# Two 1024-wide products in a row over neighbouring PSUM banks, and TensorE's order as a written list

## The chip, the cores and the metric

The kernel runs on one core of a Trainium2 chip. The metric is the device time of one execution in microseconds (us). A core has five engines with a queue of instructions each: TensorE (PE in the profile, with its weight loads as PEld), VectorE (DVE), ScalarE (ACT), GpSimd (POOL) and SyncE (SP, which issues transfers here). Each engine takes its queue in order; an instruction can wait for events of other engines, and then everything behind it on that engine waits too.

## The reference

Two stages. The first is attention through 32 inducing points, the second a gated feed-forward layer on its result.

```
x: 4 x 12416 x 128     inducing: 32 x 128
mab(q, kv): a = softmax(q @ kv.T / sqrt(128)) ; return a @ kv
h   = mab(inducing, x)          # 32 x 128 for each of the 4 batches
y   = mab(x, h)                 # 12416 x 128 for each batch
out = (sigmoid(y @ w_gate) * (y @ w_val)) @ w_out
                                # w_gate, w_val: 128 x 1536, w_out: 1536 x 128
```

## The kernel before

The attention weights of a token over the 32 inducing points are called a2. Since y = a2 @ h, the kernel never forms y: for each batch it makes hw, that is h @ w_gate and h @ w_val (32 rows each), and a hidden value is a2 @ hw, a matmul that contracts over 32 rows. The sigmoid is written as (1 + tanh(g/2)) / 2.

The unit of the main loop is a **chunk**: 512 tokens (one of 97 blocks) by 128 hidden columns (one of 12). A chunk needs a matmul for the gate (`g_ps`, 128x512 in PSUM), a matmul for the value (`v_ps`), ScalarE's tanh of the gate (`t`), VectorE's product u = (t + 1) * v, which reads `v_ps` straight from PSUM, and four 128x128 matmuls of u with w_out that add into `acc_ps`. When the 12 chunks of a block are in, ScalarE copies `acc_ps` out times one half (`o`), and SP sends it. There are 1164 chunks; 9 of the last batch go *aside* (tanh and copy on ScalarE, product on GpSimd), so VectorE makes 1155.

Chunks go in **steps** that alternate between two chunks and one. PSUM has eight banks of 512 fp32 columns: two for a double gate, one for a single gate, two for a double value, one for a single value, one for `acc_ps`, and one, `m`, that everything else shares in turn. So VectorE's products alternate between 128x1024 and 128x512. Two steps, three chunks, are a **slot**.

The order around them is written by a Python loop, the same for every step t: `product(t)` issues the value matmuls of step t, behind them the gate matmuls of step t + 2, then the product; `gate(t + 2)` issues the tanh; at odd t `project` issues 12 or 16 of the output matmuls. Other work is hung on slot numbers by `at(slot, make)`. It is: stage 1 for the next batch (scores of the inducing points over x, max, exp, sums), joining the groups into h and hw, and stage 2 (scores s2, their exponentials `e`, GpSimd's sums and inverse, the spread `a2n`, and a transposing transfer `a2r` that the gate and value matmuls of 48 chunks read). A stage 2 table entry gives the slots of its scores, of ScalarE's copy `sc`, and of its exponential.

Gate and value matmuls of a chunk sit in different row tiles of the array: rows 0 to 63 hold the gate's (even and odd hidden column blocks 32 rows each), rows 64 to 127 the value's. A product of two chunks has a no-op ahead of it on VectorE that takes its wait for the tanh.

Of the kernel before, what the change touches and what calls it, by code (L numbers as in the profile page):

```python
# [16 lines left out]
P = 128  # L18
GC = 16
BC = 4  # L20
ASIDE = {3: ((2, 9, 3, 8), (11, 17, 7, 1), (23, 26, 7, 0), (50, 53, 15, 3), (58, 62, 19, 11), (64, 69, 19, 10), (73, 76, 20, 5), (78, 81, 23, 11), (83, 88, 23, 10))}
LATE = (4, 19, 32, 46, 43)
# [11 lines left out]
TINY = 1.0e-9 / P  # L34


@with_exitstack
def kernel(
# [31 lines left out]
    up = ctx.enter_context(tc.tile_pool(name="up", bufs=6))  # L70
    tp = ctx.enter_context(tc.tile_pool(name="tp", bufs=4))
    op = ctx.enter_context(tc.tile_pool(name="op", bufs=4))
# [145 lines left out]

    summed = [0] * B
    def keep_on(n, tag):  # L220
# [9 lines left out]
    plan = {}  # L230

    def at(slot, make, late=False, side=False):
        plan.setdefault((slot, "side" if side else late), []).append(make)
# [15 lines left out]
    def s1_score_pe(b, s, tag, s1=None):  # L249
        c0, n = groups[s]  # L250
        ng, w, R = s1_dims(s)
        if s1 is None:
            s1 = ps.tile([P, 512], F32, tag=tag, name="s1_ps")
        for g in range(ng):
            nc.tensor.matmul(  # L255
                s1[32 * g : 32 * g + 32, 0 : w * P],
                indT[:],
                xT[b][:, c0 + g * w : c0 + (g + 1) * w, :].rearrange("c j t -> c (j t)"),
                start=True,
                stop=True,  # L260
            )
        return s1

    def s1_max(b, s, s1):
        ng, w, R = s1_dims(s)
        nm, _, col = s1_col(b, s)
        nc.vector.tensor_reduce(  # L267
            out=nm[0:R, col], in_=s1[0:R, 0 : w * P], axis=AX.X, op=ALU.max, negate=True
        )
# [6 lines left out]
    def s1_exp(b, s, s1):  # L276
# [3 lines left out]
        nc.scalar.activation(  # L280
# [5 lines left out]
        )  # L286
        return a1T

    def s1_turn_pe(b, s, a1T, tag="m"):
        ng, w, R = s1_dims(s)  # L290
        aT = ps.tile([P, 4, P], F16, tag=tag, name="aT_ps")
        for k in range(w):
            nc.tensor.transpose(aT[:, k, 0:R], a1T[0:R, ts(k, P)], ident[0:R, 0:R])
        return aT

    def s1_turn_copy(s, aT):
        ng, w, R = s1_dims(s)
        a1 = s1p.tile([P, 4, P], F16, tag="a1")
        nc.vector.tensor_copy(out=a1[:, 0:w, 0:R], in_=aT[:, 0:w, 0:R])
# [7 lines left out]
    def s1_sum_pe(b, s, a1, hp, k0, k1):  # L307
        c0, n = groups[s]
        ng, w, R = s1_dims(s)
        for k in range(k0, min(k1, w)):  # L310
            for cols, src in ((slice(0, C), None), (slice(C, C + 1), ones16[:])):
                for g in range(ng):
                    if b == 0 and src is not None:
                        continue
                    nc.tensor.matmul(  # L315
# [6 lines left out]
                    )  # L322

    def s1_sum_keep(b, s, hp):
# [5 lines left out]
        nc.scalar.copy(out=hsts[b % 2][0:R, at_col[s], 0:width], in_=hp[0:R, 0:width])  # L330

    def plan_stage1(b, s, score, total):
        st = {}
        full = groups[s][1] == GC

        def begin():
            st["s1"] = s1_score(b, s, "m")

        def weigh():
            st["a1T"] = s1_exp(b, s, st["s1"])  # L340

        def turn():
            if full:
                st["a1"] = s1_turn_dma(b, s, st["a1T"])
            else:
                st["a1"] = s1_turn_copy(s, s1_turn_pe(b, s, st["a1T"]))

        at(score, begin)
        at(score + 1, weigh, late=full)
        at(score + 2, turn)  # L350
        first, second, keep = total

        def part(k0, k1):
            if k0 == 0:
                st["hp"] = ps.tile([P, C + 1], F32, tag="m", name="hp_ps")
            s1_sum_pe(b, s, st["a1"], st["hp"], k0, k1)

        at(first, lambda: part(0, 2))
        at(second, lambda: part(2, 4))
        at(keep, lambda: s1_sum_keep(b, s, st["hp"]))  # L360
# [12 lines left out]
    def l_inverse(l_ps):  # L373
        li = bp.tile([P, m], F32, tag="li")
        nc.vector.reciprocal(out=li[:], in_=l_ps)
        return li

    def h_take(b, h_ps, li):
        hT16[b] = bp.tile([P, m], F16, tag="hT", name="hT")
        nc.vector.tensor_tensor(out=hT16[b][:], in0=h_ps, in1=li[:], op=ALU.mult)  # L380

    def hw_fill(b, hf, tag):
        hw_ps = ps.tile([P, NI // 2, P], F32, tag=tag, name="hw_ps")
        for r in range(4):
            wsrc = wg16 if r < 2 else wv16
            nc.tensor.matmul(
# [5 lines left out]
            )  # L392
        return hw_ps
# [22 lines left out]
    def plan_combine(b, lead, weights, fill):  # L416
# [4 lines left out]
        def least():  # L421
# [3 lines left out]
            st["col"] = join_min(bp, ml)  # L425
# [27 lines left out]
        def total():  # L453
            lh = ps.tile([P, 2, m], F32, tag="m", name="lh_ps")
            nc.tensor.matmul(lh[:, 0, :], ones[:], st["e32l"][:], start=True, stop=True)
            nc.tensor.matmul(lh[:, 1, :], st["hx"][:, 0, 0:C], e32[:], start=True, stop=True)
            st["lh"], st["li"] = lh, l_inverse(lh[:, 0, :])

        def part(hf):
            st["hw_ps"] = hw_fill(b, hf, "m")  # L460

        def keep(hf):
            if hf == 0:
                st["hwt"] = bp.tile([P, NI, P], F16, tag="hw", bufs=B, name="hwt")
            nc.scalar.copy(out=st["hwt"][:, ts(hf, NI // 2), :], in_=st["hw_ps"][:])
# [3 lines left out]
        at(lead, least)  # L469
        at(weights, weigh)  # L470
        at(weights + 1, join)
        at(weights + 8, total)
        at(weights + 9, lambda: h_take(b, st["lh"][:, 1, :], st["li"]))
        for hf, (first, second) in enumerate(fill):
            at(first, lambda hf=hf: part(hf))
            at(second, lambda hf=hf: keep(hf), late=True)
# [4 lines left out]
    def s2_score(b, c, j0, j1, s2, whole=False):  # L481
        for j in range(j0, j1):
            nc.tensor.matmul(  # L483
# [6 lines left out]
            )  # L490

    def s2_max(n, s2):
        nmx = s2p.tile([P, GC], F32, tag="nmx")
        nc.vector.tensor_reduce(
            out=nmx[:, 0:n], in_=s2[:, 0:n, :], axis=AX.X, op=ALU.max, negate=True
        )
# [8 lines left out]
    def s2_exp(n, s2, hi, lo):  # L505
        for t_, last in ((hi, False), (lo, True)):
            nc.tensor.matmul(
# [6 lines left out]
            )  # L514
        e = s2p.tile([P, GC + NLO, m], F16, tag="e")
        nc.scalar.activation(out=e[:, 0:n, :], in_=s2[:, 0:n, :], func=AF.Exp, scale=SCALE)
        return e

    def s2_take(sc, c0, n, s2):
        nc.scalar.copy(out=sc[:, c0 : c0 + n, :], in_=s2[:, 0:n, :])  # L520
# [96 lines left out]
    def plan_stage2(b, c, score, take, weigh, far=None, soon=False):  # L617
        st = {}
        n = GC + (NLO if far is not None else 0)

        def bank():
            st["s2"] = ps.tile([P, GC, m], F32, tag="m", name="s2_ps")
# [4 lines left out]
        def one():  # L627
            room()
            bank()
            s2_score(b, 0, 0, NLO, st["s2"], True)  # L630

        def half(j0, whole):
            if j0 == 0:
                bank()
            s2_score(b, c, j0, j0 + GC // 2, st["s2"], whole)
            if soon and j0:
                st["hl"] = s2_max(GC, st["s2"])

        def lower():
            if far is None:  # L640
                room()
            s2_take(st["sc"], 0, GC, st["s2"])
            s2_lower_pool(n, st["sc"])

        def exp():
            st["e"] = s2_exp(GC, st["s2"], *st["hl"]) if soon else s2_exp_low(n, st["sc"])

# [12 lines left out]
        if far is not None:  # L660
            at(far, one)
            at(far + 1, lambda: s2_take(st["sc"], GC, NLO, st["s2"]))
        at(score, lambda: half(0, False))
        at(score + 1, lambda: half(GC // 2, not soon))
        if not soon:
            at(take, lower, late=True)
        at(weigh, exp, late=True)
        at(weigh + 1, total)
        at(weigh + 3, spread)
        at(weigh + (5 if soon else 8 if far is None else 7), turn)  # L670
# [187 lines left out]
    s2_a = ps.tile([P, GC, m], F32, tag="m", name="s2_ps")  # L858
# [34 lines left out]
    a2T = [ps.tile([P, half, P], F16, tag=t, name="a2T_ps") for t in ("m", "v1")]  # L893
# [17 lines left out]
    steps = []  # L911
    blocks = []
    first_step = {}
    for b in range(B):
        for s in range(NG):
            first_step[(b, s)] = len(blocks) * 2 * NJ // 3
            blocks += [[(b, groups[s][0] + k, BC)] for k in range(0, GC, BC)]
    blocks.append([(b, 0, NLO) for b in range(B)])
    order = [list(range(NJ)) for _ in blocks]
    aside = []  # L920
    for b, table in ASIDE.items():
        first = b * NG * GC // BC
        for g, v, i, j in table:
            order[first + i].remove(j)
            aside.append((first * 4 + g, first * 4 + v, first + i, j))
    for i in range(len(blocks)):
        js = list(order[i])
        while js:
            cnt = 1 if steps and steps[-1]["cnt"] == 2 else 2
# [261 lines left out]
```

## Time and profile before

| | |
|---|---|
| median of 3 runs | 719.6 us (719.52 to 720.22) |
| span of the profiled execution | 718.4 us; the median of the runs is 1.2 us longer, taken as what lies around the span |
| VectorE busy | 702.4 us (98%), 872 instructions |
| ScalarE busy | 675.1 us (94%), 1019 instructions |
| TensorE busy (matmul) | 650.5 us (91%) |
| GpSimd busy | 445.8 us (62%) |
| products on VectorE | 385 of 128x1024, 384 of 128x512, the last cut in two |

The page gives no other time for the profiled execution than its span, so sums are made against the span plus 1.2 us. Busy time of an engine is the union of its instructions; the mean length of one instruction is longer than its share of that, where each begins before the one ahead of it has ended. "Idle before" in a group's row is the time in which the engine did nothing just ahead of these instructions, with what ended most of it.

### The profile page before, as it was taken

What the parts mean: (1) busy time and instruction counts of PE and PEld (TensorE: products, weight loads), DVE (VectorE), ACT (ScalarE), POOL (GpSimd) and SP (SyncE); (2) the same over time, 40 slices, a digit from 0 to 9 for tenths busy, and PEclk for the clock granted to TensorE, in tenths of its full rate; (3) what the DMA queues carried; (4) which work ended last, traced back from release to release, by engine and by line L of the source; (5) the groups of instructions that cost most, each with busy time, mean ns of one, the idle gap of its engine ahead of it and who ended that gap; (6) DMA issues with size and microseconds to landing.
All of it is one profiled execution on the core that took longest, in us unless ns stands there. A gap on an engine that the chain in (4) does not pass through costs nothing.

```text
span 718.4 us, 21566 instructions
## 1 busy us (share of the span) xinstructions
PE 650.5 (91%) x8446; PEld 394.2 (55%) x8446; DVE 702.4 (98%) x872; ACT 675.1 (94%) x1019; POOL 445.8 (62%) x718
## 2 busy tenths in 40 slices
PE   8889889999998998999989988999899999999897
PEld 4455555555555555555555555555555555555555
DVE  5899999999999999999999999999999999999997
ACT  4699999999999999999999999999999999999996
POOL 4574763888653747588666266387766787676220
PEclk9999999999999999999999999999999999999999
DMA  9796696244568344335268431220222122223011
GB/s 209 115 182 130 125 165 105 75 90 106 89 133 162 80 103 92 59 79 119 66 117 161 102 75 51 70 74 31 77 60 73 46 62 67 39 75 71 35 46 46
DMA packets 118182, 65.77 MB, mean 92 GB/s; under 512 B 101408, under 2 KB 102208, under 8 KB 118080
## 3 DMA queue, kind: packets, MB, share of 16 engines
q1 hardware_dynamic: 112176, 50.90, 31.6%
q0 software_dynamic: 5584, 13.34, 10.9%
q8 instruction: 66, 1.08, 0.6%
q14 instruction: 36, 0.29, 0.1%
q10 hardware_dynamic: 320, 0.15, 0.1%
HBM read 27.80 MB, written 25.43 MB: 74 GB/s over the span
## 4 chain that ended last, share of the span: by engine, by line
PE 51%; ACT 24%; DVE 16%; issue 5%; DMA 2%; DVEq 1%; POOL 1%; ACTq 0%
PE acc_ps L1062 24%; ACT t L962 22%; PE v_ps L944 21%; DVE u L981 14%; PE g_ps L944 2%; DMA xn<-in_x_dram 2%; PE s_ps L483 2%; PE hp_ps L315 1%; ACT o L1081 1%; DVE nm L267 1%; DVEq L981 1%; ACT a1T L280 0%; PE s_ps L255 0%; POOL xn L96 0%; ACTq L962 0%
## 5 line engine op out<-in xcount | busy, mean ns | idle before, releaser
L981 DVE SCALAR_TENSOR_TENSOR u<-t,v_ps 128x1024 f16<-128x1024 f16 (+1 forms) x771 | 670.9, 945 | 1.7 <-PE g_ps L944 0.8
L962 ACT ACTIVATE t<-g_ps 128x1024 f16<-128x1024 f32 (+1 forms) x770 | 589.5, 822 | 22.2 <-ACT t L962 10.3
L944 PE MATMUL v_ps<-a2r,hwt 32*128 32x512 f16 (+1 forms) x1179 | 290.8, 371 | 56.9 <-DVE u L981 53.2
L1062 PE MATMUL acc_ps<-wo,u 128*128 128x128 f16 x4620 | 324.5, 220 | 0.9
L1062 PEld LDWEIGHTS <-u 128*128 128x128 f16 x4620 | 259.9, 98 | 89.5 <-issue 88.1
L944 PE MATMUL g_ps<-a2r,hwt 32*128 32x512 f16 (+1 forms) x1179 | 294.0, 376 | 0.0
L944 PEld LDWEIGHTS <-hwt 32*128 32x128 f16 x2382 | 93.5, 91 | 188.6 <-issue 142.2
L552 POOL TENSOR_TENSOR sum<-e 128x256 f32<-128x256 f16 (+1 forms) x23 | 15.5, 672 | 133.8 <-ACT e L544 130.0
L598 POOL TENSOR_TENSOR a2n<-e,rs 128x2048 f16<-128x2048 f16 (+3 forms) x25 | 86.8, 3474 | 4.8 <-DVE rs L570 3.1
L576 POOL TENSOR_TENSOR near<-sme,minus 128x16 f32<-128x16 f32 (+1 forms) x22 | 65.3, 2966 | 1.8
L1081 ACT ACTIVATE o<-acc_ps 128x512 f32<-128x512 f32 x96 | 58.4, 609 | 0.0
L531 POOL TENSOR_SCALAR rise<-rise 128x256 f32<-128x256 f32 (+6 forms) x110 | 51.2, 466 | 9.7
L532 POOL TENSOR_TENSOR top<-top,rise 128x128 f32<-128x128 f32 (+3 forms) x88 | 28.4, 323 | 7.3
L552 POOL TENSOR_TENSOR sum<-sum 128x128 f32<-128x128 f32 (+3 forms) x92 | 28.4, 309 | 7.2
L530 POOL TENSOR_TENSOR rise<-top 128x128 f32<-128x128 f32 (+3 forms) x88 | 27.3, 310 | 6.9
L530 POOL TENSOR_TENSOR rise<-sc 128x256 f32<-128x256 f32 (+1 forms) x22 | 16.3, 739 | 20.9 <-ACT sc L520 20.6
L1031 POOL TENSOR_TENSOR xn_spare<-xn_spare 128x512 f16<-128x512 f32 x9 | 11.4, 1270 | 22.2 <-ACT xn_spare L1029 22.0
L535 POOL TENSOR_TENSOR sc<-sc,top 128x512 f32<-128x512 f32 (+1 forms) x22 | 23.9, 1086 | 1.7
L1026 POOL TENSOR_SCALAR xn_spare<-xn_spare 128x512 f32<-128x512 f16 x9 | 13.4, 1493 | 11.2 <-ACT xn_spare L1025 11.2
L483 PEld LDWEIGHTS <-xT 128*128 128x128 f16 x388 | 13.1, 96 | 11.7 <-issue 11.3
L280 ACT ACTIVATE a1T<-s_ps,nm 128x512 f16<-128x512 f32 (+1 forms) x26 | 16.4, 630 | 3.1 <-DVE nm L267 3.0
L483 PE MATMUL s_ps<-hT,xT 128*128 128x32 f16 x388 | 18.1, 178 | 0.1
(150 smaller groups left out, 291.4 us busy)
## 6 DMA issues: line engine op xcount, KB each, us to landing
out_dram<-o SPq DMA_DIRECT2D x96, 256.0 KB, 2.2
xn<-in_x_dram POOLq DMA_DIRECT2D x18, 512.0 KB, 7.7
xn<-in_x_dram POOLq DMA_DIRECT2D x3, 544.0 KB, 6.9
xn<-in_x_dram POOLq DMA_DIRECT2D x3, 256.0 KB, 12.8
xn<-in_x_dram SPq DMA_DIRECT2D x1, 576.0 KB, 4.8
xn<-in_x_dram SPq DMA_DIRECT2D x1, 512.0 KB, 3.9
a2r<-a2n SPq DMA_TRANSPOSE x29, 4.5
wg<-in_moe_w_gate_dram POOLq DMA_DIRECT2D x1, 384.0 KB, 12.7
```

The lines of the kernel that those rows point to most:

```text
L483: nc.tensor.matmul(s2[:, j, :], xT[b][:, c + j, :], hT16[b][:], start=(j == 0), stop=whole and j == j1 - 1, skip_group_check=True,)
L530: nc.gpsimd.tensor_tensor(out=r, in0=far, in1=near, op=ALU.subtract)
L531: nc.gpsimd.tensor_scalar_max(out=r, in0=r, scalar1=0.0)
L532: nc.gpsimd.tensor_tensor(out=top[:, 0:n, 0:w], in0=near, in1=r, op=ALU.add)
L552: nc.gpsimd.tensor_tensor(out=d[:, 0:n, :], in0=src[:, :, 0:w], in1=src[:, :, w : 2 * w], op=ALU.add)
L576: nc.gpsimd.tensor_tensor(out=near[:, 0:n], in0=sme[:, 0:n], in1=minus1[:, 0:n], op=ALU.pow)
L598: eng.tensor_tensor(out=a2n[:, 0:n, :, :], in0=e.unsqueeze(2).to_broadcast((P, n, 4, m)), in1=rs.unsqueeze(2).unsqueeze(3).to_broadcast((P ...
L944: st[what + "end"] = nc.tensor.matmul(pt[:, k, col : col + nb * P], hw[b][r : r + 32, j // 2, :], a2r[r : r + 32, o : o + nb, :].rearrange ...
L962: st["tanh"] = nc.scalar.activation(out=st["t"][:], in_=st["g"][:], func=AF.Tanh, scale=0.5)
L981: u = nc.vector.scalar_tensor_tensor(out=st["u"][:, :, c:e], in0=st["t"][:, :, c:e], scalar=1.0, in1=st["v"][:, :, c:e], op0=ALU.add, op1= ...
L1062: nc.tensor.matmul(acc[0][(i // 2) % len(acc[0])][:, i, :], u[:, ts(i, P)], wo16[:, j, :], start=(i in fresh), stop=not any(e[2] == ib and ...
L1081: nc.scalar.mul(out=o32[:], in_=acc[0][0][:], mul=0.5)
```

## The change

Bank `m` and the single value bank become one tile `vm` of two neighbouring banks. In a slot in which no other work holds `m`, the second product is 128x1024 over both banks of `vm`; in the others it is 128x512 in the first bank, and `m` serves as before. Words in a long text, `ORDER`, now say what is issued next: `V` or `W` value matmuls (a `W` at a slot's start makes its second product wide), `x` the product, `g` a gate's matmuls with its tanh, `o8` eight output matmuls, `p`, `a` and `d` other work on TensorE, ScalarE and VectorE. Gates still alternate between two chunks and one, and their tanh goes into one ring of 16 chunks. Blocks begin with even or odd hidden columns in turn so that pairs fit. Slots in the tables (`TIMES`) become chunk positions (three per slot), and several moved by one or two; the nine aside chunks stay nine, from other places of the order. Buffers for u go from 18 chunks to 16, those for the copied-out block from 4 to 3. `on` tells the scheduler that users of one bank of `vm` need not wait for users of the other.

```diff
+    vm.append(ps.tile([P, 2, 512], F32, tag="vm", name="vm_ps"))
...
-    def product(t):
-        st = steps[t]
-        hidden_mm(st, "v")
...
-        gate_fill(t + 2)
-        if t % 2:
-            beside(t // 2, "side")
...
+    def fill_value():
+        c, n, half = value["chunk"], sizes[value["step"]], value["step"] % 2
+        if half == 0:
+            turn_page(c)
+        v = vm[0] if half else ps.tile([P, 2, 512], F32, tag="v2", name="v_ps")
+        for k in range(n):
...
+            for i in hidden_mm("v", c + k, v[:, k, :]):
...
+    def product():
...
+        cuts = [0, 384, 512] if final else [0, 512]
+        for a, e in zip(cuts, cuts[1:]):
+            x = nc.vector.scalar_tensor_tensor(
+                out=u[:, 0:n, a:e],
+                in0=ring[:, p : p + n, a:e],
+                scalar=1.0,
+                in1=v[:, 0:n, a:e],
...
+ORDER = """
+ggVxggVxpVxgVxo4ggVxgVxpo12gVd0xo8go4gVxo4Vxgo4a0gVxo8Wxo4a0gVxgo12gWxo4gVxo12gVxgo8pgVxpo4a0gWx
...
+    for word, k in words:
+        if word in "VW":
+            fill_value()
+        elif word == "x":
+            product()
+        elif word == "g":
+            issue_gate()
+        elif word == "o":
+            for _ in range(int(k)):
+                out_mm()
+        else:
+            run(later[{"p": "pe", "a": "act", "d": "dve"}[word]].pop(int(k or 0)))
```

VectorE's queue in the second batch of tokens, before: u is the product, t the tanh, and the size is that of the result.

```order
L981 SCALAR_TENSOR_TENSOR u_3341<-t_3311,v_ps 128x512
L981 SCALAR_TENSOR_TENSOR u_3365<-t_3335,v_ps 128x1024
L981 SCALAR_TENSOR_TENSOR u_3395<-t_3343,v_ps 128x512
L981 SCALAR_TENSOR_TENSOR u_3417<-t_3368,v_ps 128x1024
L981 SCALAR_TENSOR_TENSOR u_3434<-t_3397,v_ps 128x512
```

And a like stretch of VectorE's queue with the change; `t_621` is the ring.

```order
L1350 SCALAR_TENSOR_TENSOR u_3323<-t_621,vm_ps 128x1024
L1350 SCALAR_TENSOR_TENSOR u_3337<-t_621,v_ps 128x1024
L1350 SCALAR_TENSOR_TENSOR u_3368<-t_621,vm_ps 128x512
L1350 SCALAR_TENSOR_TENSOR u_3386<-t_621,v_ps 128x1024
L1350 SCALAR_TENSOR_TENSOR u_3406<-t_621,vm_ps 128x1024
```

Every second product was 128x512; now 164 of the 330 slots have two of 128x1024 (four chunks), and 166 have one of each. Together that is 661 products where there were 770, for the same 1155 chunks; in the last batch 166 where there were 194. VectorE's other instructions are as many as before, and so are ScalarE's 770 tanh instructions.

TensorE's queue in a slot without other work, before (`v_ps` value, `g_ps` gate, `acc_ps` output matmul; weight loads and like rows left out):

```order
L944 MATMUL v_ps_4138<-a2r_3626,hwt_560 128x512
...
L944 MATMUL g_ps_4141<-a2r_3626,hwt_560 128x512
...
L944 MATMUL v_ps_4149<-a2r_3626,hwt_560 128x512
...
L944 MATMUL g_ps_4151<-a2r_3626,hwt_560 128x512
...
L1062 MATMUL acc_ps_4072<-wo16_105,u16_4091 128x128
...
L1062 MATMUL acc_ps_4072<-wo16_105,u16_4102 128x128
```

And with the change, a slot of four chunks and the head of a slot of three, with other work in bank `m` (`vm_ps<-hT,xT` are scores of stage 2):

```order
L1120 MATMUL v_ps_3741<-a2r_3379,hwt_563 128x512
...
L1249 MATMUL acc_ps_3747<-wo16_108,u16_3704 128x128
...
L1120 MATMUL g_ps_3756<-a2r_3379,hwt_563 128x512
...
L1120 MATMUL vm_ps_533<-a2r_3379,hwt_563 128x512
...
L1249 MATMUL acc_ps_3747<-wo16_108,u16_3720 128x128
...
L1120 MATMUL g_ps_3773<-a2r_3379,hwt_563 128x512
...
L1120 MATMUL v_ps_3778<-a2r_3379,hwt_563 128x512
...
L1120 MATMUL g_ps_3788<-a2r_3379,hwt_563 128x512
...
L650 MATMUL vm_ps_533<-hT_3173,xT_1_97 128x32
```

Each step's value and gate matmuls stood together, with all output matmuls of a slot in one run of 12. Now groups of gate and value matmuls are cut by runs of four or eight output matmuls: there are 662 such groups and 620 runs of output matmuls, where there were 770 steps and 384 runs. A gate's matmuls can stand apart from any value's.

More of the change, by code (lines that the diff above doesn't have):

```diff
@@ L363 @@
+        sums[b] = sums.get(b, []) + [chain(
+            b - 1,
+            (first, "take", lambda: part(0, 2), WIDE, 290),
+            *([(None, "pe", lambda: part(2, 4), WIDE, 290)] if full else []),
+            (None, "act give", put, C),
+            needs=[(scores, len(scores["steps"]))],
+        )]
     hT16 = {}
```

718 lines of the change are left out of this document (461 added, 257 removed).

## The prediction

> **What bounds the kernel now.** I read the page's busy times first, then the busy time by stretches, then the groups with their shapes, then the waits, and last some microseconds of the timeline. The page and two stretches, the first three batches from 60 us on and the last batch:
>
> ```profile
> PE 650.5 (91%) x8446; PEld 394.2 (55%) x8446; DVE 702.4 (98%) x872; ACT 675.1 (94%) x1019; POOL 445.8 (62%) x718
> ...
> 60.00:540.00 480.00, 436.86 (x5830) 265.75 (x5829) 479.96 (x573) 463.35 (x696) 312.65 (x518) 1.00 0.46 96
> 540.00:710.00 170.00, 158.44 (x1910) 95.80 (x1909) 168.83 (x194) 166.24 (x247) 101.51 (x137) 1.00 0.21 54
> ```
>
> In the rows of stretches the columns behind the length are PE, PEld, DVE, ACT and POOL. VectorE is busy for 479.96 of 480 us: it sets the time of the first three batches alone, and of its 16 idle us nearly all lie before 30 us and behind 710. ScalarE is idle for 16.7 us of those 480. In the last batch, with nine chunks aside on ScalarE and GpSimd, it is idle for 3.8 of 170, against 1.2 for VectorE: two engines are near their limit there. The granted clock is 1.00 in both.
>
> ```profile
> L981 DVE SCALAR_TENSOR_TENSOR u<-t,v_ps 128x1024 f16<-128x1024 f16 x385 | 467.5, 1214 | 1.7 <-PE g_ps L944 0.8 <-PE v_ps L944 0.2
> L962 ACT ACTIVATE t<-g_ps 128x1024 f16<-128x1024 f32 x385 | 398.5, 1035 | 22.1 <-ACT t L962 10.3 <-PE g_ps L944 4.9
> L981 DVE SCALAR_TENSOR_TENSOR u<-t,v_ps 128x512 f16<-128x512 f16 x384 | 260.6, 679 | 0.0
> ...
> L981 DVE SCALAR_TENSOR_TENSOR u<-t,v_ps 128x1024 f16<-128x1024 f16 (+1 forms) x771 | 670.9, 945 | 1.7 <-PE g_ps L944 0.8
> ```
>
> The last of these rows has all products together. They cover 670.9 us, less than the 728.1 of the two rows by shape, since each begins before the one ahead has ended. VectorE waits only 1.7 us for anything ahead of them. TensorE waits for VectorE instead, to get a value bank back:
>
> ```profile
> PE v_ps L944 <- DVE u L981: 54.1, 223, 0.8
> ```
>
> **What VectorE saves.** 512 columns more make a product 1214 - 679 = 535 ns longer. The 1155 chunks thus hold 1155 x 0.535 = 617.9 us of streaming; the other 53.0 of the 670.9 us are 69 ns for each of 771 instructions. A stretch of ten products, five of each width, says the same:
>
> ```profile
> 299.59 8.73 DVE L981 SCALAR_TENSOR_TENSOR u<-t,v_ps 128x1024 f16<-128x1024 f16 x10
> ```
>
> 8.73 - 15 x 0.535 = 0.70, or 70 ns each, with the drain of the last one in it. The change removes 770 - 661 = 109 products: 109 x 0.069 = 7.5 us, of which 81 (5.6 us) in the first three batches and 28 (1.9 us) in the last. I price a wide product over `vm` like one over the double value buffer, since that is two banks too; at worst the second bank costs the fixed part again, and the gain is 0.
>
> The Trainium skill, "VectorE: DVE Perf Modes", section "The TRN2 errata", gives a VectorE instruction with a PSUM source 120 cycles besides one for each column at 0.96 GHz, that is 125 ns where I take 69. By it the sum would be 109 x 0.125 = 13.6 us. The trace does not agree: 771 x 0.125 + 617.9 would be 714 us of products, where 670.9 were measured.
>
> **ScalarE.** It keeps 770 tanh instructions, its copies and the nine chunks aside: nothing is removed. In the first three batches its 16.7 us of idle time take the 5.6. In the last batch 3.8 us would have to shrink to 1.9. Part of this idle time comes from tanh waiting for a gate bank that TensorE filled late (the row above: 10.3 us put down to ScalarE's own events, 4.9 to TensorE). With the gates written 4 to 6 chunks ahead of the values, where they were 3 ahead, it can shrink, but not to nothing. Bounds 0 and 1.9; I take half, 1.0, as the idle time is twice what is asked of it.
>
> **TensorE.** The same matmuls, cut otherwise. A stretch with no wait in it:
>
> ```profile
> 303.21 0.38 PE L944 MATMUL v_ps<-a2r,hwt 32*128 32x512 f16 x1
> 303.22 0.39 PE L944 MATMUL g_ps<-a2r,hwt 32*128 32x512 f16 x1
> ...
> 303.53 0.67 PEld L1062 LDWEIGHTS <-u 128*128 128x128 f16 x12 [0.23 <-issue]
> 303.54 0.84 PE L1062 MATMUL acc_ps<-wo,u 128*128 128x128 f16 x12
> ...
> 304.31 0.39 PE L944 MATMUL v_ps<-a2r,hwt 32*128 32x512 f16 x2
> 304.32 0.39 PE L944 MATMUL g_ps<-a2r,hwt 32*128 32x512 f16 x2
> 304.64 0.36 PE L483 MATMUL s_ps<-hT,xT 128*128 128x32 f16 x8
> ```
>
> Two fills take 303.54 - 303.21 = 0.33 us, and four fills in four row tiles also 304.64 - 304.31 = 0.33. Twelve output matmuls take 0.77, of which 12 x 0.056 (0.67 for twelve weight loads) is the run and 0.10 the switch back. Before: 770 x 0.33 + 384 x 0.10 = 292 us besides the output matmuls themselves. With the change: 662 groups, which hold 813 rounds if a row tile used twice in a group begins another, so 662 to 813 x 0.33, and 620 x 0.10 for the switches: 280 to 330. TensorE's work grows by -12 to +38 us, and the 54.1 us in which it waited for VectorE cover this and the 7.5 us by which the time shrinks. At the upper bound 8.6 us are left of that cover. I take 0 on the path, and come back to it under the rivals.
>
> The Trainium skill, "TensorE: Matmul & The Clock Gate", "Part 3: Packing small matmuls", has matmuls in different row tiles overlap, so that a pack lasts one matmul and some 4 ns for each further tile. The two 0.33 us above agree, and the rule speaks against this change: a gate group that no longer stands with a value group costs a span of its own.
>
> **Other waits.** Where a slot is narrow, the next double value bank must be filled while a 512 product runs (0.60 us: 679 less the overlap), as before; where it is wide, while a 1024 product runs (1.14), which is easier. The first matmuls of a new group need its transposed weights. The tightest of these places in the middle batches:
>
> ```profile
> 304.03 3.61 POOL L598 TENSOR_TENSOR a2n<-e,rs 128x2048 f16<-128x2048 f16 x1
> 307.67 1.86 SPq L609 DMA_TRANSPOSE a2r<-a2n  x1
> ...
> a2r<-a2n SPq DMA_TRANSPOSE x29, 4.5
> ...
> 315.21 1.02 ACT L962 ACTIVATE t<-g_ps 128x1024 f16<-128x1024 f32 x1 [0.22 <-ACT t L962]
> ```
>
> Issued at 307.67 and landed 4.5 later, at 312.2, for a tanh at 315.21 whose gate fill begins some 0.5 earlier: 2.5 us to spare. In ScalarE's queue 36 chunks of tanh stood between that group's exponential and its first tanh; now there are 34, so some 1.2 us of the 2.5 go. It still holds at the median landing; the three middle places (one in each of the first three batches) cost between 0 and 1 us each if it does not. I take 0.5 us for all new waits together, nearest to none.
>
> The buffers for u hold 16 chunks, and output matmuls trail products by 5 to 8 chunks in the order: no cost. The beginning and the tail (last products, 16 output matmuls, two halves out) keep their form: no change.
>
> **The sum.** 718.4 - 5.6 - 1.0 + 0.5 = 712.3 us of span, and with the 1.2 us around it 713.5, against the median of 719.6. Its own range: at best all 7.5 us and VectorE's 1.7 us of waits go, 710.4; at worst nothing in the last batch and 3 us at the late transposes, 717.0.
>
> **The rivals.**
>
> *ScalarE sets the pace.* Its 22.1 us of idle time ahead of tanh do not shrink, because each gate fill stands at a written place in TensorE's queue and arrives when TensorE gets there. For: 98% busy in the last batch. Against: 16.7 us free before it, and gates further ahead. A third of the 7.5 us comes through: 719.6 - 2.5 = 717.1, between 716.0 and 718.2.
>
> *The change gives nothing*: a product over the two banks of `vm` pays as much as two, 719.6. Against it is the row of 1214 ns over two banks already.
>
> *A value group comes late in narrow slots: slower.* VectorE now takes its products without a pause because TensorE waits for the bank and fills it at once. With the change a gate group (0.33 us) or a run of four output matmuls (0.22 + 0.10) stands ahead of some value group, and a gate group can itself be held by ScalarE; only 0.60 us of a 512 product covers the fill of 0.33 that follows. A late one costs VectorE up to 0.33 us. 7.5 / 0.33 = 23 late ones of the 166 narrow slots cancel the gain; if one slot in three is hit, 55 x 0.33 = 18.2, and 719.6 - 6.1 + 18.2 = 731.7. For it: the upper bound of TensorE's work leaves 8.6 us of 54.1, and in the last batch TensorE is busy for 158.4 of 170. Against it: in the middle of TensorE's range half of the cover remains, and the wide slots give each fill more time.
>
> *Each product that goes takes its whole recorded overhead along.* A 512 product is recorded 679 - 535 = 144 ns longer than its columns stream; if none of that overlapped, 109 x 0.144 = 15.7 us would go, and 719.6 - 15.7 = 703.9. The 670.9 us against 728.1 speak against it, and so do ScalarE's 3.8 us in the last batch. The Trainium skill's section on the errata, above, has 125 ns for this, and 706.0.
>
> **How the numbers follow.** Forecast 0.65; ScalarE's pace 0.10; the whole overhead 0.01; no gain 0.06; late value groups 0.18, from a few late ones (721 to 722, 0.03 of the 0.18) to the 731.7. A measurement of this kernel tells about 0.2% from no change, 1.4 us. Faster by more than that is the first three cases, 0.76; within it 0.06; slower 0.18. The range goes from 710.4, the forecast's best, to 722.0: it leaves out 0.15 of late value groups, 0.01 below, and 0.03 for the forecast's own edges.
>
> **What would show it.** Right: 494 products 1024 wide at 1214 ns and 167 of 512 at 679, VectorE busy near 695 us and again for all but 1 us between 60 and 540; TensorE's wait for VectorE down from 54.1 to between 8 and 58; ScalarE idle for about 11 us in the first three batches. Wrong: idle time of VectorE ahead of products, put down to value matmuls (late groups) or to tanh (ScalarE's pace); waits of gate matmuls for a transfer; a mean above 1214 for the wide product over `vm`.

## The result and the profile after

The change makes the kernel slower: 726.6 us median of 4 runs (723.7 to 728.8) against 719.6, a ratio of 1.0094 with a 95% interval of 1.0069 to 1.0118. The profiled execution has a span of 721.9 us, with 1.8 us around it; before it was 718.4.

The page's busy times after, and the busy time by stretches, with the same columns as before and one stretch more, 30 to 60 us:

```profile
PE 684.1 (95%) x8446; PEld 401.4 (56%) x8446; DVE 701.4 (97%) x763; ACT 679.2 (94%) x1019; POOL 445.9 (62%) x718
...
30.00:60.00 30.00, 28.30 (x312) 15.46 (x311) 28.68 (x33) 27.98 (x41) 18.21 (x30) 0.94 0.87 158
60.00:540.00 480.00, 459.75 (x5789) 269.63 (x5785) 476.16 (x493) 463.99 (x692) 310.30 (x513) 1.00 0.46 96
540.00:710.00 170.00, 163.54 (x1893) 96.43 (x1891) 168.94 (x166) 166.90 (x247) 102.53 (x142) 1.00 0.20 56
```

VectorE has 109 instructions fewer and is busy only 1.0 us less, 701.4 where some 695 were forecast; and in the first three batches it is idle for 3.8 of 480 us, where it was 0.04. ScalarE's idle time there is 16.0 us, hardly less than 16.7. TensorE is busy 33.6 us longer. The row of 30 to 60 us has a granted clock of 0.94 (its last three columns are this clock, the DMA share and GB/s).

The groups by shape, and the waits that answer to the one shown of before:

```profile
L1350 DVE SCALAR_TENSOR_TENSOR u<-t,v_ps 128x1024 f16<-128x1024 f16 x330 | 400.6, 1214 | 4.1 <-PE v_ps L1120 1.2 <-PE g_ps L1120 0.6 <-ACT t L1163 0.3
L1350 DVE SCALAR_TENSOR_TENSOR u<-t,vm_ps 128x1024 f16<-128x1024 f16 x164 | 199.1, 1214 | 0.9 <-PE vm_ps L1120 0.5
L1350 DVE SCALAR_TENSOR_TENSOR u<-t,vm_ps 128x512 f16<-128x512 f16 x166 | 112.8, 679 | 1.5 <-ACT t L1163 0.5 <-PE vm_ps L1120 0.4 <-issue 0.2
L1163 ACT ACTIVATE t<-g_ps 128x1024 f16<-128x1024 f32 x385 | 397.4, 1032 | 17.8 <-ACT t L1163 4.1 <-PE v_ps L1120 2.6 <-PE g_ps L1120 2.3
```

```profile
PE g_ps L1120 <- ACT t L1163: 7.1, 29, 0.5
PE v_ps L1120 <- DVE u L1350: 4.6, 13, 0.7
...
PE g_ps L1120 <- DMA a2r<-a2n: 1.6, 2, 0.9
...
PE vm_ps L1120 <- DVE u L1350: 0.9, 5, 0.2
```

A wide product costs 1214 ns over either tile. TensorE now waits at gates for ScalarE, and for VectorE only 5.5 us instead of 54.1. One such place in the timeline:

```profile
192.31 1.02 ACT L1163 ACTIVATE t<-g_ps 128x1024 f16<-128x1024 f32 x1
192.50 1.21 DVE L1350 SCALAR_TENSOR_TENSOR u<-t,v_ps 128x1024 f16<-128x1024 f16 x1
192.63 0.39 PE L1120 MATMUL vm_ps<-a2r,hwt 32*128 32x512 f16 x2
193.23 0.59 ACT L1274 ACTIVATE o<-acc_ps 128x512 f32<-128x512 f32 x1
193.39 0.39 PE L1120 MATMUL g_ps<-a2r,hwt 32*128 32x512 f16 x2 [0.36 <-ACT t L1163]
193.63 1.21 DVE L1350 SCALAR_TENSOR_TENSOR u<-t,vm_ps 128x1024 f16<-128x1024 f16 x1
...
193.88 0.61 PE L1249 MATMUL acc_ps<-wo,u 128*128 128x128 f16 x8
194.41 0.38 PE L1120 MATMUL g_ps<-a2r,hwt 32*128 32x512 f16 x1
194.42 0.39 PE L1120 MATMUL v_ps<-a2r,hwt 32*128 32x512 f16 x2
...
194.88 1.22 DVE L1350 SCALAR_TENSOR_TENSOR u<-t,v_ps 128x1024 f16<-128x1024 f16 x1
```

The double gate bank is held by the tanh of 192.31 until 193.33. TensorE stands at that gate for 0.36 us; eight output matmuls and the values are queued behind it. The values come at 194.42, and the third product starts 1.25 us after the second, where the second started 1.13 us after the first. The loss is 0.12 us, but VectorE's record shows only 0.04 of idle time (193.63 + 1.21 = 194.84): the first 0.08 goes into the overlap that two products in a row otherwise have.

So lateness has to be read from spacing, not from idle time. An undisturbed 1024 product ends 1.13 us after the one ahead, a 512 one 0.60. Summed over all pairs of products in a row between 60 and 700 us, the time beyond that is 3.6 us before (33 products more than 20 ns late) and 12.0 after (100, of them 86 wide). Nearly all of this lateness comes by way of the values: of the 97 products that are late by over 25 ns with the change, 93 (11.1 of 11.9 us) start at most 0.6 us behind the start of their last value matmul, while their tanh had ended 2.6 us earlier in the median. So TensorE's queue brings the values late.

What held the queue is less plain. Call a **hold** the time by which a matmul starts later than it does behind the same neighbour when nothing is awaited (3 ns behind one in another row tile, 220 in the same, 152 behind an output matmul, 317 from a gate or value to an output matmul). A hold of over 150 ns at a gate group stands within the 2.5 us ahead of 47 of the 97 late products, but also of 220 of the 486 that are on time; by itself it tells nothing. Better evidence, though no proof: from 81 of the late products, back to the last place at which TensorE was held at values (where it was ahead of VectorE), the holds at gates add up to at least the lateness in 65.

The account of the profiled executions: four chunks take 2 x 1131 = 2262 ns in two products and 1131 + 2 x 598 = 2327 in three, so that 109 products fewer at 65 ns are -7.1 us; late products are +8.4; the start is +1.2, by the end of the product that completes chunk 48 (VectorE is busy for 28.68 of the 30 us ahead of 60, at the clock of 0.94). Together this is +2.5, where the span grew by 3.5; 1.0 us is not assigned. The median lies 2.9 us above the profiled execution's time. It goes with the clock: the four runs had mean clocks of 0.996, 0.992, 0.990 and 0.988 and took 723.7, 726.8, 726.4 and 728.8 us; the runs of the kernel before beside the experiments had 0.998 to 1.0.

### The profile page after: what moved, and what is told of

It is laid out like the page before. It is cut to its first block, busy times and chain, and to the rows that moved or that the text cites. A ratio compares the mean times of both kernels' runs of the same rounds, so it can differ in the third digit from the quotient of the medians.

```text
span 721.9 us, 21194 instructions
## 1 busy us (share of the span) xinstructions
PE 684.1 (95%) x8446; PEld 401.4 (56%) x8446; DVE 701.4 (97%) x763; ACT 679.2 (94%) x1019; POOL 445.9 (62%) x718
## 4 chain that ended last, share of the span: by engine, by line
PE 52%; ACT 23%; DVE 10%; issue 9%; POOL 3%; DMA 2%; ACTq 0%; DVEq 0%; POOLq 0%
PE acc_ps L1249 25%; ACT t L1163 18%; PE g_ps L1120 13%; DVE u L1350 10%; PE v_ps L1120 5%; PE vm_ps L1120 4%; ACT o L1274 3%; DMA xn<-in_x_dram 2%; PE vm_ps L650 1%; PE vm_ps L427 1%; DMA a2r<-a2n 1%; ACT e L711 1%; ACT a1T L392 1%; POOL a2n L765 1%; PE vm_ps L367 0%
## 5 line engine op out<-in xcount | busy, mean ns | idle before, releaser
L1350 DVE SCALAR_TENSOR_TENSOR u<-t,v_ps 128x1024 f16<-128x1024 f16 (+1 forms) x332 | 401.4, 1209 | 4.1 <-PE v_ps L1120 1.2
L1249 PE MATMUL acc_ps<-wo,u 128*128 128x128 f16 x4596 | 364.2, 220 | 6.6 <-ACT o L1274 1.1
L1249 PEld LDWEIGHTS <-u 128*128 128x128 f16 x4620 | 265.2, 98 | 152.7 <-issue 145.1
L1350 DVE SCALAR_TENSOR_TENSOR u<-t,vm_ps 128x512 f16<-128x512 f16 (+1 forms) x330 | 311.9, 945 | 2.4 <-PE vm_ps L1120 0.9
L1120 PE MATMUL g_ps<-a2r,hwt 32*128 32x512 f16 (+1 forms) x1179 | 287.9, 375 | 13.8 <-ACT t L1163 6.9
L1120 PEld LDWEIGHTS <-hwt 32*128 32x128 f16 x2382 | 97.1, 91 | 128.2 <-issue 55.9
L1120 PE MATMUL v_ps<-a2r,hwt 32*128 32x512 f16 (+1 forms) x677 | 127.2, 374 | 6.4 <-DVE u L1350 4.6
L1120 PE MATMUL vm_ps<-a2r,hwt 32*128 32x512 f16 (+1 forms) x502 | 126.3, 377 | 1.2 <-DVE u L1350 0.9
```

The lines of the kernel that those rows point to most:

```text
L1120: made_mm.append(nc.tensor.matmul(out[:, col : col + nb * P], hw[b][r : r + 32, j // 2, :], a2r[r : r + 32, o : o + nb, :].rearrange("p j ...
L1249: mm = nc.tensor.matmul(acc[0][half][:, i, :], u[:, ts(i, P)], wo16[:, j, :], start=(i in fresh), stop=not left[ib] and not any(e[1] == ib ...
L1350: x = nc.vector.scalar_tensor_tensor(out=u[:, 0:n, a:e], in0=ring[:, p : p + n, a:e], scalar=1.0, in1=v[:, 0:n, a:e], op0=ALU.add, op1=ALU ...
```

## The experiments

| run | us, median | ratio, 95% interval | mean clock of the profiled run |
|---|---|---|---|
| values ahead of gates | 738.6 | 1.0238 to 1.0291 | 0.988 |
| fewer output matmuls | 724.3 | 1.0047 to 1.0081 | 0.990 |
| before, gate group first | 722.2 | 1.0019 to 1.0043 | 0.995 |
| before, runs of output matmuls cut | 721.6 | 1.0017 to 1.0040 | 1.0 |
| list by a rule, wide | 848.6 | 1.1766 to 1.1814 | 0.912 |
| the same, gates further ahead | 840.6 | 1.1633 to 1.1694 | 0.912 |
| list by a rule, no wide slot | 771.0 | 1.0685 to 1.0732 | 0.964 |
| gates later | 757.8 | 1.0486 to 1.0608 | 0.995 |
| short tanh | 720.6 | 0.9997 to 1.0038 | 0.995 |
| short tanh, fewer output matmuls | 729.1 | 1.0092 to 1.0137 | 0.971 |
| short tanh, early fill | 718.4 | 0.9963 to 1.0003 | 0.997 |
| before, short tanh | 717.0 | 0.9950 to 0.9974 | 1.0 |
| short tanh, more output matmuls | 727.4 | 1.0086 to 1.0116 | 0.998 |
| change, more output matmuls | 737.0 | 1.0218 to 1.0244 | 1.0 |

Ratios are to the kernel before, run on the same chip, where its median was 719.7 to 720.0 us, and 720.4 for the last two rows.

### Values ahead of gates, and gates later

Where gate words stand directly ahead of a value word, they go behind it.

```diff
+    order_text = re.sub(r"(g+)([VW])", r"\2\1", ORDER.replace("\n", ""))
```

> The changed kernel; in its written order each group of gate matmuls that stands directly ahead of a value group goes behind it. Theory A (order in the queue): a gate group waits for ScalarE to free its bank and holds the value group behind it, so this brings back part of the loss: 716 to 722 us, and TensorE's gates wait more, VectorE less. Theory B (amount of TensorE work: more and shorter runs leave it no room): the number of groups and runs is the same, so no change, 725 to 728 us. Theory C (a wide product over the two banks costs VectorE more): no change.

Measured 738.6 us, 12.0 more than the change and outside what all three theories expected. The waits of this run:

```profile
ACT t L1164 <- PE g_ps L1120: 13.1, 32, 1.5
PE v_ps L1120 <- DVE u L1351: 9.4, 31, 0.7
DVE u L1351 <- PE g_ps L1120: 8.7, 15, 1.6
```

TensorE now waits for VectorE's banks first, and the gates behind come late: ScalarE waits 13.1 us for gate matmuls (2.9 with the change), and VectorE for the products that need them. Merely swapping the two doesn't help; the gates are needed as early as they stand. The opposite move puts 89 gate groups behind the output matmuls that follow them:

```diff
+    order_text = re.sub(r"xg(o\d+)(?=[VW])", r"x\1g", ORDER.replace("\n", ""))
```

> The changed kernel; in its list 89 gate groups that stand ahead of one run of output matmuls and then a value group move behind that run. Number of groups and runs unchanged. Theory A: fewer waits for ScalarE, 722 to 725 us against 726.6. Theory B or C: no change.

Measured 757.8 us, again outside all that was expected. Waits:

```profile
PE g_ps L1120 <- ACT t L1164: 24.0, 64, 1.0
ACT t L1164 <- PE v_ps L1120: 15.9, 24, 1.8
```

ScalarE starves and is then behind, and TensorE waits for it more often than with the change. The theory that gates merely stand too early has fallen: neither of these two moves cures the loss at them.

### The kernel before with one part of the new order

In the first run `gate_fill(t + 2)` goes ahead of the values in `product`; in the second the output matmuls of a slot are issued in two runs, four behind the even step.

```diff
     def product(t):
         st = steps[t]
+        gate_fill(t + 2)
         hidden_mm(st, "v")
...
-        gate_fill(t + 2)
```

> The kernel before, in which the gate matmuls of step t + 2 stand ahead of the value matmuls of step t instead of behind them; nothing else. Theory A: slower, 723 us or more, with idle time of VectorE ahead of products. Theories B and C: no change, 719 to 721 us.

```diff
+        if t % 2 == 0 and acc[0] is not None:
+            n = len(queue)
+            project(t - 1, t, BC)
+            early[:] = [n - len(queue), acc[0] is None]
...
```

> The kernel before with its run of 12 output matmuls cut into 4 (between the two steps of a slot) and 8: as many groups and runs as the changed kernel has (about 550 and 540 from the loop's first part on), values still ahead of gates, products still 1024 and 512. Adds 0.2 us a slot, about 53 us of TensorE work, less the waits it fills. Theory B: slower, 724 us or more. Theory A: 719 to 722 us, with TensorE's wait for VectorE much smaller. Theory C: no change.

722.2 and 721.6 us. The wait of TensorE for VectorE, first run, then second:

```profile
PE v_ps L944 <- DVE u L981: 9.5, 18, 0.6
```

```profile
PE v_ps L944 <- DVE u L985: 21.7, 66, 0.7
```

The first run takes 45 of the 54.1 us away and is 2.5 us slower, the second 32 and 1.9. In the regular order of before the cover works as the prediction put it: what is added eats the wait. In the first run most of the increase, 1.6 us, arises in the first 24 chunks, where the clock was at half for 6.8 us. Its row of the first three batches:

```profile
60.00:540.00 480.00, 466.24 (x5829) 264.05 (x5823) 479.79 (x573) 462.53 (x696) 312.11 (x518) 1.00 0.45 96
```

TensorE is busy for longer than with the change (459.75), ScalarE hardly less, and VectorE still goes without a pause. So neither TensorE's busy time nor a gate ahead of the values is by itself what costs the change its gain. Holds of over 0.1 us between 60 and 700 us add up, before, to 8 us at gates and 109 at values; in this run to 43 and 76; with the change to 53 and 26. The two orders hold the gates nearly alike, but TensorE is far less often ahead of VectorE with the change. That this is the difference that counts fits the runs; none of them isolates it.

### Lists written by a rule

Three lists of words were generated by a simple rule like the loop of before (values, gates up to three or four chunks ahead, product, other work, then one run of output matmuls): two with 214 wide slots, one with none.

> The changed kernel with another written list, made by the rule of the kernel before: a value group, right behind it the gates (until they stand 3 chunks ahead), the product, other work, and then one run of output matmuls (8 a product in wide slots, 12 a slot in narrow ones). Slots are wide wherever the shared bank is free: 627 products where the change has 661 and the kernel before 770. Theory A (the list: gates written too early and apart make TensorE wait in front of values): VectorE sets the time again, 143 x 0.065 = 9.3 us off 719.7, 710 to 714. Theory B (two-chunk products against gates of two and one are themselves the trouble): 719 us or more. Theory C (the clock, which falls to one half for some microseconds in runs of the change): it falls here too, and the time is spread by several us from run to run.

> As the run before, with gates 4 chunks ahead instead of 3, nothing else. Theory A: between it and the change, 1 to 4 us slower than lead 3, as a gate written earlier waits longer for ScalarE. Theory B: no difference between the two leads.

> As e5, but no slot is wide: products 1024 and 512 in turn, as in the kernel before, with the ring, the two-bank tile, the buffers and the chunk positions of the change. Control for the rest of the change: 719 to 721 us if these cost nothing, 723 or more if they do.

848.6, 840.6 and 771.0 us. The list without wide slots was to be the control, and is 51 us slower than before, so the three say nothing on wide slots. A reason shows in its waits:

```profile
PE vm_ps L1118 <- DVE u L1348: 46.0, 178, 0.8
...
DVE u L1348 <- PE g_ps L1118: 27.1, 44, 1.7
ACT t L1161 <- PE g_ps L1118: 23.7, 46, 1.5
ACT t L1161 <- ACT t L1161: 20.6, 87, 0.6
ACT a1T L390 <- DVE nm L377: 16.8, 23, 2.1
```

The last row was 3.0 us, 2 times, before: the rule puts the exponential of stage 1 directly behind the maximum it needs, and ScalarE and all behind it stand for 0.7 us 23 times. What the rest is was not followed up; the clock was low in all three (0.912 to 0.964).

### Less work for ScalarE

Each tanh covers 448 of 512 columns; the other 64 of the ring hold a constant and no gate. This takes some 48 us from ScalarE (679.2 to 631.6 busy) and leaves every queue's order as it is.

```diff
+    nc.gpsimd.memset(ring[:, :, 448:], 0.0)
...
-            out=ring[:, p : p + n, :], in_=g[:, 0:n, :], func=AF.Tanh, scale=0.5
+            out=ring[:, p : p + n, 0:448], in_=g[:, 0:n, 0:448], func=AF.Tanh, scale=0.5
```

> The changed kernel; each tanh of the main loop covers 448 of the 512 tokens of a chunk (the last 64 read a constant instead, so their output is not the reference's). By the mean lengths, 1032 and 608 ns, a chunk streams 424 ns, so ScalarE gets 1155 x 0.125 x 0.424 = 61 us less work, some 9%; TensorE's list and VectorE's products stay. Theory D (ScalarE, 97% busy, frees gate banks too late for the written places, and the value groups behind them come late): the forecast's 711 to 714 us appear. Theory E (the order is wrong by itself: value groups come late however soon ScalarE is done): 720 us or more.

720.6 us, which would be the number of Theory E, but the first product waited 4.0 us for the constant to be written. At the product that completes chunk 24 this run is about 5 us behind the kernel before, at chunk 1152 level with it: in between it gains about 5 where the change loses nearly 3. So the constant was written early on VectorE instead, and the kernel before got the same short tanh as a control.

> The change with each tanh over 448 of its 512 columns, as in the last but one, but the constant in the other 64 columns is written once on VectorE near the start, in an idle stretch, so that the first product waits for nothing new. All queues keep their order. Theory (ScalarE frees the gate banks late, TensorE waits for them in its queue, and the value groups behind come late): the loop gains 5 us on the kernel before, as it did from chunk 24 on with the late fill, and the time is 714 to 717; TensorE's waits at gates for ScalarE stay near 2.5 us. Rival (TensorE's own work, 49 us more in the loop, sets the pace, and the earlier run only looked better because its late start gave the other engines a lead): 720 to 724, and late products as many as with the full tanh.

> Control: the kernel before with the same shorter tanh, over 448 of 512 columns, its constant columns also written near the start; all queues keep their order. Theory (the kernel before is bound by VectorE alone, ScalarE's pace matters only with the change): 717.5 to 719.8, since at most the few late products (3.6 us) can go; the change is then worth 2 to 5 us against this control where it cost 7 with the full tanh. Rival (ScalarE's load costs both kernels alike): the control gains as much as the change does from the shorter tanh, 8 us or more, and comes in at 712 or below.

The change with the short tanh: 718.4 us median, its profiled run 715.8. The control: 717.0, half a microsecond below what was expected of it. The page's busy times of both and, from the waits, TensorE's for the other two engines; first the change:

```profile
PE 681.4 (95%) x8446; PEld 401.1 (56%) x8446; DVE 697.2 (98%) x764; ACT 631.7 (88%) x1019; POOL 444.8 (62%) x718
```

```profile
PE v_ps L1122 <- DVE u L1351: 7.0, 23, 0.7
...
PE g_ps L1122 <- ACT t L1164: 2.3, 9, 0.4
```

And the control:

```profile
PE 640.0 (89%) x8446; PEld 387.9 (54%) x8446; DVE 701.3 (98%) x880; ACT 621.8 (87%) x1019; POOL 444.7 (62%) x718
```

```profile
PE v_ps L951 <- DVE u L990: 65.8, 269, 0.8
```

TensorE's wait at gates falls from 7.1 to 2.3 us, and the lateness of products from 12.0 to 5.1 us. Eleven of the twelve runs of the change lie near a line in the mean clock: 714.1 us at 0.999, 716.5 at 0.997, 718.6 at 0.992, 723.1 at 0.983, or 0.54 us for each 0.001 and 714.5 at a clock of 1.0 (the twelfth, 729.1 at 0.986, lies above it). The four runs of the change itself give 0.58 and 721.4. By these lines, the second of which rests on four points and is carried beyond them, the shorter tanh is worth 6.9 us to the change at full clock; to the kernel before it is worth 2.7. The 4.2 us between them are what ScalarE's load costs the change alone: about half of the 7.9 us between the 713.5 forecast and 721.4. The expected median was 714 to 717; by the line, the clock is why it came out at 718.4.

### Less and more work for TensorE

Output matmuls of two of the twelve column blocks are left out: 776 of them, at 56 ns 43 us.

```diff
     def out_mm():
         nonlocal fresh
         u, ib, j, i = queue.pop(0)
+        if j in (5, 6):
+            return
```

> The changed kernel without the output matmuls of hidden column blocks 5 and 6 (2 of 12; those columns are missing from the output), which takes 776 x 0.056 = 43 us of work from TensorE and leaves everything else in place. Theory B: VectorE becomes the bound again and the forecast's 712 to 714 us appear. Theory A: what is late waits for ScalarE, not for the amount of work, so most of the loss stays, 721 to 726 us. Theory C: no change, 726 us.

> As e9, and without the output matmuls of hidden column blocks 5 and 6 as in e2: ScalarE has 61 us and TensorE 43 us less to do. Theory D: 711 to 713 us, like e9 or 1 us better. Theory B (TensorE's work, hidden behind ScalarE in e2): e9 stays near 724 and this one falls to 711 to 713. Theory E: 718 us or more in both.

724.3 us, only 2.2 less than the change, and with the short tanh (late fill) 729.1, more than without the cut. In both the clock falls. Two stretches of the first run, ahead of and in one piece of half clock, and its two main waits:

```profile
455.80:459.20 3.40, 2.04 (x18) 0.95 (x17) 2.58 (x4) 1.72 (x3) 0.00 (x0) 1.00 0.49 132
459.20:466.00 6.80, 6.79 (x51) 3.48 (x48) 4.78 (x6) 5.29 (x9) 0.00 (x0) 0.52 0.10 20
```

```profile
PE g_ps L1120 <- ACT t L1163: 20.7, 69, 0.6
PE v_ps L1120 <- DVE u L1352: 10.8, 32, 0.8
```

TensorE is busy for 2.04 of 3.4 us, and the clock is then at half for 6.8 us, in which VectorE is idle for 2.0. In the run with both cuts four such pieces last 41 us together. On a line in the clock, the four runs of the first kernel give 718.3 us at 1.0: 43 us less work are worth 3.1 us to the change, and the rest of TensorE's saving turned into waits, of 20.7 us for ScalarE and 10.8 for VectorE. Adding work tests the other direction: 384 more output matmuls, over a block of zeros (nothing is added to the sum), 21.5 us.

```diff
+        if j == 5 and more and i not in fresh and not final:
+            nc.tensor.matmul(
+                acc[0][half][:, i, :],
+                u[:, ts(i, P)],
+                z16[:],
+                start=False,
+                stop=False,
+                skip_group_check=True,
+            )
```

> As the run with the short tanh and the early fill, with 384 output matmuls more, of u with a block of zeros (four in a block of tokens, each behind the matmul whose weights it has), at 56 ns each 21.5 us of TensorE's time. Theory (the half-clock pieces come from stretches in which TensorE streams too little, and make the runs of that kernel scatter from 714 to 723 at 0.5 us for each 0.001 of mean clock): the mean clock rises from its 0.993 to 0.997 or more, the scatter shrinks, and the median is 714 to 718, so not worse than its 718.4 although TensorE has 21.5 us more to do. Rival (the clock falls for another reason, and TensorE's work is itself on the path): the clock stays at 0.993 or lower and the time rises by 5 us or more, to 723 or over.

> The change as it is, with the same 384 output matmuls over zeros. Theory of the clock, as above: the mean clock rises from 0.9915 to 0.996 or more; a full-clock time of 721.4 for the change (its runs carried on to a clock of 1.0 at 0.58 us for each 0.001) plus what the late gates lose by TensorE's added work, 721 to 727. Rival (TensorE's work is on the path with the full tanh, as the gates leave it no room): 730 or over, with TensorE's waits at gates shrinking by as much as work is added or not, and VectorE's late products growing.

727.4 and 737.0 us. The clock of the change rises to 1.0 in four of five runs, which lie within 0.8 us of each other: the scatter goes away. But the time rises, by 15.6 us over the 721.4 at full clock, of which 0.8 is the chip (the kernel before took 720.4 on it): some 15 us for 21.5 of work. With the short tanh the median rises by 9.0 us (8.3 without the chip's part) and the clock to 0.994 to 0.998 in five of six runs; the sixth took 740.6 at 0.988. That TensorE's work is on the path, as both rivals said, is right; that the clock falls for another reason, as one of them said, is not. The theory is right about the clock, and with the full tanh about the scatter, but not about the time. TensorE's wait at gates, and VectorE's group, in the change with more output matmuls:

```profile
PE g_ps L1122 <- ACT t L1165: 7.8, 30, 0.5
```

```profile
L1361 DVE SCALAR_TENSOR_TENSOR u<-t,v_ps 128x1024 f16<-128x1024 f16 x330 | 401.2, 1216 | 8.8 <-PE v_ps L1122 2.5 <-PE g_ps L1122 2.2 <-ACT t L1165 0.7
```

The wait at gates takes up none of the added work (7.1 with the change). VectorE's idle time ahead of these products doubles (4.1), and the lateness of all pairs goes from 12.0 to 24.2 us.

Of the versions that compute the whole, none beats the kernel before.

## Why the prediction was wrong

**The bound and the price of a product: right.** 494 products of 1024 at 1214 ns, over `vm` too, and 167 of 512 at 679. The saving was 65 ns for each product that went, 7.1 us for 7.5. The gain was there, and was taken back elsewhere.

**TensorE, "I take 0 on the path": the step that failed.** The 54.1 us of waits for VectorE were to cover all that TensorE's order adds, as one pool. They did not: 93 of the 97 late products got their values late, the lateness grew by 8.4 us, and the price at the margin, taken as 0, is some 15 us for 21.5 of added work. Taking 43 us of work away gave back only 3.1 at full clock, so it is not the amount of work alone. How much the work grew is not settled: TensorE is busy for 33.6 us longer, near the upper bound of -12 to +38, but the run with the gate group first shows that busy time holds waiting as well, and estimates from the spacing of matmul starts lie between 10 and 60 us, by what is counted as a hold. Why the cover failed is argued, not shown: a wait covers only work that is queued at its place. In the order of before nearly all holds lie ahead of values (109 us of them), and there added work eats them (32 to 45 us of waits for 1.9 and 2.5 us of time); with the written list only 26 us at values are left. The run with the gate group first, with 43 us of holds at gates and hardly any loss, shows that holds at gates do little harm while many are left at values.

**ScalarE, half of the last batch's 1.9 us: too small.** Its idle time was counted as room. But the place of a gate in TensorE's queue is written: where ScalarE frees a gate bank late, as at 193.33, TensorE stands there though ScalarE has 3% idle time. With 48 us less work on ScalarE 6.9 us come back, 4.2 more than in the kernel before. That its idle time in the first three batches is 16.0 and not about 11 is no second finding: with the same work in a time that did not shrink it could not fall.

**Other waits, 0.5 us.** Two gate groups wait 1.6 us for a transposing transfer: the size was off, but little; what these waits cost in time was not measured.

**The rivals.** The one on late value groups had the mechanism, down to a gate group held by ScalarE. It had the place half right: 43 of the 100 late products are wide ones behind a 512 product, a third of the 129 such places between 60 and 700 us, as it supposed; the other 57 stand behind a wide product, where it saw more time. Its price of 0.33 us for a late group was too high (0.12 on average) and its count too low. It set 0.18 on a time from 721 to 731.7, and 726.6 lies in that. The range, up to 722.0, left most of it out; the row quoted for it, TensorE busy for 158.4 of 170 us in the last batch beside ScalarE's 166.2, was weighed only against the sum of the waits. The rival on ScalarE's pace saw that a gate fill stands at a written place in TensorE's queue, and had this cost two thirds of the gain, not more than all of it.

**What no step had: the clock.** The granted clock of before is 1.00 in the rows quoted, and the prediction took it to stay. By the line in the clock, pieces of half clock cost the change 2 to 7 us a run (721.4 against 723.7 to 728.8).

## What to carry to other kernels

Do not take the waits of an engine as one pool of cover. What they cover seems to depend on where in its queue they lie (argued here, not isolated), so where a change spreads the engine's work over other places, ask what waits are left ahead of the work that the bound engine needs next. Busy shares near the top are no sign either way: with TensorE, ScalarE and VectorE at 96, 97 and 99% in the first three batches the change lost, and the regular order with the gate group first, at 97, 96 and 100%, hardly did. Measure the price at the margin by adding a known amount of harmless work to the engine said to be free: 21.5 us on TensorE cost some 15. And judge lateness on a bound engine by the spacing of its instructions, since their overlap swallows the first 80 ns before any idle time shows.

## What the runs showed of the hardware

The clock of TensorE goes to half, in pieces of 3.4 us or multiples of it, behind a stretch in which TensorE streams little. In the profiled runs of the change, of the two versions with fewer output matmuls, and of those with values ahead of gates and gates later, every such piece that begins after 30 us, the last microseconds of the kernel aside, follows 3.4 us in which the columns streamed would fill at most 0.42 of the time at full clock (a matmul counted by its share of the array, a gate or value matmul as a quarter, as it has one of four row tiles), where the median is 0.53 to 0.59. Stretches as low (0.36 to 0.41) also passed without it, in the kernel before too, so what exactly releases it stays open. More streaming took it away: with 5% more matmuls the clock was 1.0 in four of five runs. So less work for TensorE can be slower: with the short tanh, the cut of 43 us made 720.6 into 729.1.

The Trainium skill, "TensorE: Matmul & The Clock Gate", "Part 1: The HAM clock gate (the "warmup" mystery)", gives windows of 3413 ns and the half rate; the pieces here agree. Its rule, in the same part, against gaps of over some 3.4 us in which TensorE is idle is not enough here: the row of 2.04 busy us in 3.40, of the change with fewer output matmuls, stands ahead of a half-clock piece, and the longest wait in it was this one:

```profile
457.34 0.39 PE L1120 MATMUL g_ps<-a2r,hwt 32*128 32x512 f16 x2 [1.36 <-DMA a2r<-a2n]
```

What its section "A second HAM failure mode: psum-queue depth-cycling" says, that short pauses between groups of matmuls can also bring the clock down, is nearer to this row; that page puts them down to cycling through PSUM banks, which no run here tests.
